# Where the last output wait stands: SyncE's wait moved past the end of the block, the first output moved to ScalarE's queue

## The chip, the cores and the metric

One core of a Trainium2 chip runs the kernel. The metric is device time in microseconds (us), the median of several executions. The *span* is the time from the program's first instruction to its last; the steps that the runtime adds behind the program are called its ending here.

## The reference, cut to what matters

The same decode attention runs twice, on inputs A and B (8 sequences, 32 heads, 4096 cached positions, head size 128, bf16), and the two results stand side by side.

```
q = (x @ wq) split into 32 heads
p = softmax(q . k_cache^T / sqrt(128))
o = p . v_cache
out = o (heads joined: 4096) @ wo          # 8 x 1 x 1024
return concatenate([out_A, out_B], axis=-1)   # 8 x 1 x 2048
```

The caches are read once: the page accounts for 1107 MB read from memory and 0.03 MB written.

## The kernel before

SyncE issues every load but the two small inputs x, which ScalarE issues. The last loads are `wo` of A, then `wo` of B in four pieces, so that the last projection can start before all of it is there. For each cache the projection ends in one cast from PSUM (the memory that the matmuls write) into `orow` on VectorE and one 16 KB store. In the code `c` is 0 for A and 1 for B (`NC` is 2); `add` and `dma` enter an operation together with the list of those that it waits for.

```python
        orow = sb("orow", [128, DT], BF16)
# ... make_proj(c), after the matmuls of cache c:
            opEv[c] = add("dve", lambda e: e.tensor_copy(orow[:], proj[:, 0:DT]), [opProj[c]] + outs)
            outs.append(dma(out[:, 0, c * D:(c + 1) * D].rearrange("b (q n) -> q b n", q=NT), orow[0:128:32 // B, :],
                            ("out", 0), [opEv[c]], "sp"))
# ... the end of the program:
        P.run("sp", nc.sync, sems, part=(0, 2))
        block = es.enter_context(nc.Block())

        @block.sync
        def _(eng):
            P.run("sp", eng, sems, part=(2, None))
            eng.wait_ge(sems[("out", 0)], counts[("out", 0)])
# ... the other four engines alike, without a wait
```

Three things matter. `opEv[1]` waits for the first store, because both casts write the same `orow`. The first store goes onto SyncE's queue behind the pieces of `wo`. And SyncE waits for both stores *inside* the block; the end of a block is a barrier over all five engines: none goes on before all have arrived.

## Time and profile before

| | before |
|---|---|
| time, median of 3 runs before the prediction | 2564.28 us (2564.10 to 2564.41) |
| span of the profiled run | 2562.854 us |
| last piece of `wo` landed | 2559.807 us |
| last output landed | 2562.461 us |
| end of the block's barrier, which is the end of the span | 2562.854 us |
| last step of the runtime's ending in the trace | 2564.814 us |

The page first: busy time by engine, the DMA rows over the span in 40 slices, and the DMA queues (packets, MB, share of 16 engines' time).

```profile
span 2562.9 us, 18832 instructions
PE 1118.5 (44%) x7712; PEld 397.1 (15%) x7712; DVE 2170.2 (85%) x1042; ACT 129.9 (5%) x401; POOL 2.6 (0%) x15
...
DMA  9999999999999999999999999999999999999999
GB/s 425 427 438 430 437 431 437 431 437 431 436 432 435 433 435 433 435 433 433 435 430 435 432 436 432 436 431 436 432 436 432 436 432 435 432 435 433 434 433 394
...
q1 hardware_dynamic: 19512, 1107.34, 99.9%
...
q10 hardware_dynamic: 32, 0.03, 0.0%
```

The DMA engines are busy for at least nine tenths of every slice: the kernel is bound by its loads. Queue 1 is SyncE's, queue 10 ScalarE's, which carries only the two inputs x. A change that leaves the loads alone can move only the ends.

The end of the chain of waits (start us, us, what):

```profile
2520.56 39.25 DMA ring<-in_B_wo_dram
2559.81 0.04 issue
2559.85 0.36 PE proj L431 x4
2560.21 0.02 issue
2560.24 0.42 DVE orow L435
```

The timeline of the last stretch (start us, us, engine, line, operation):

```profile
2559.22 0.97 PE L431 MATMUL proj<-ring,on_sb 128*32 128x256 bf16 x16 [0.28 <-DMA ring<-in_B_wo_dram]
2559.85 0.15 PEld L431 LDWEIGHTS proj<-ring,on_sb 128*32 128x32 bf16 x4 [0.32 <-DMA ring<-in_B_wo_dram]
2560.24 0.42 DVE L435 CAST orow<-proj 128x256 bf16<-128x256 f32 x1 [13.59 <-PE proj L431]
2560.69 0.54 SPq L208 DMA_DIRECT2D out_dram<-orow  x1
```

And SyncE's own waits from 2540 us on (us in total, times, longest):

```profile
SPq L208 <- DVE orow L435: 39.0, 2, 25.7
SPq L162 <- DMA out_dram<-orow: 1.2, 1, 1.2
SPq L162 <- PEq L162: 0.2, 1, 0.2
```

Line 208 is the helper that issues DMAs; line 162 stands for the end of the block. The reader is to see a strict sequence: last piece of `wo`, four matmuls, cast, store, 1.2 us of waiting for the store, and *then* the barrier (0.2 us of waiting in it). The views above stop at the program's last instruction. The trace's semaphore record goes on. It lists when each semaphore, the counter by which engines and transfers signal each other, was updated; no view of `prof` prints it (us, semaphore; 111 counts the outputs, 2 belongs to the runtime):

```
2561.647 sem 111      2562.402 2562.407 2562.416 2562.461 sem 111
2563.093 2563.127 2563.334 2563.378 2563.402 2563.507 2563.546 2563.580 2563.627 sem 2
  (the semaphores are reset)
2564.457 2564.491 2564.529 2564.573 2564.597 2564.695 2564.733 2564.767 2564.814 sem 2
```

Each store updates its semaphore once and then four times more. The Trainium skill says why in "DMA: Bandwidth & Descriptors", section "Why a DMA increments its semaphore by 16 and not by 1": a copy runs on the largest number of engines, up to 16, that divides the slowest dimension of both its sides. Here these are 32 and 4, so four engines. By the same section each engine adds one when its data have landed, and the issuing sequencer writes the remaining count immediately. The trace agrees in the number of updates: one at 2561.647, four later. It does not record their sizes.

The nine steps on semaphore 2 are what the skill's page "Runtime: NRT & Kernel Launch", section "The ~15µs preamble/postamble breakdown", calls a sync barrier, "the actual serpentine across 5 engines", at 44 ns a hop and about 355 ns in all. Nine steps fit a signal that passes over five engines and back, with the fifth step as the turn; the e5 runs below bear this out. The last nine steps of this trace take 357 ns, with single hops of 24 to 98 ns. The first nine take 534 ns, mostly because the third comes 207 ns after the second instead of 38.

### The profile page before, as it was taken

To read this page: it belongs to the slowest core of one execution; us is meant where nothing else is said; L and a number is where in the kernel's file an instruction comes from. 1 tells how busy PE (TensorE), PEld (TensorE's weight loads), DVE (VectorE), ACT (ScalarE), POOL (GpSimd) and SP (SyncE) were. 2 spreads that over 40 slices of the span, in tenths; PEclk is the share of its full clock that TensorE was granted. 3 is DMA by queue.
4 is the path that set the end of the run, shared out by engine and by line. 5 is a ranking of instruction groups with operands and counts; after the bars stand their busy time and mean duration, and the time that the engine had idled before them with its cause. 6 is when DMAs were issued, how large, how long until landed. Compare 5 with 4: busy or idle time off the path is not lost.

```text
span 2562.9 us, 18832 instructions
## 1 busy us (share of the span) xinstructions
PE 1118.5 (44%) x7712; PEld 397.1 (15%) x7712; DVE 2170.2 (85%) x1042; ACT 129.9 (5%) x401; POOL 2.6 (0%) x15
## 2 busy tenths in 40 slices
PE   2443443443443444444444434444444444434435
PEld 1111111111111111111111111111111111111112
DVE  3898898898898898898898888888988988988983
ACT  1100000000000000000000000000000000000000
POOL 0000000000000000000000000000000000000000
PEclk7676776677766766766766767666666767667676
DMA  9999999999999999999999999999999999999999
GB/s 425 427 438 430 437 431 437 431 437 431 436 432 435 433 435 433 435 433 433 435 430 435 432 436 432 436 431 436 432 436 432 436 432 435 432 435 433 434 433 394
DMA packets 19555, 1107.51 MB, mean 432 GB/s; under 512 B 2185, under 2 KB 2249, under 8 KB 2521
## 3 DMA queue, kind: packets, MB, share of 16 engines
q1 hardware_dynamic: 19512, 1107.34, 99.9%
q8 instruction: 7, 0.11, 0.0%
q10 hardware_dynamic: 32, 0.03, 0.0%
q14 instruction: 4, 0.02, 0.0%
HBM read 1107.33 MB, written 0.03 MB: 432 GB/s over the span
## 4 chain that ended last, share of the span: by engine, by line
DMA 52%; DVE 28%; issue 16%; PE 4%; ACT 0%; DVEq 0%; SPq 0%; ACTq 0%
DMA ring<-in_A_k_cache_dram 25%; DMA ring<-in_B_k_cache_dram 25%; DVE ring L330 10%; DVE ring L335 10%; PE red L345 4%; DVE s_sb L353 4%; DVE PM L370 3%; DMA ring<-in_B_wo_dram 2%; DVE rmax L359 1%; DVE rtmp L360 0%; ACT PM L291 0%; DVEq L135 0%; PE o L285 0%; DVE ngm L363 0%; SPq L208 0%
## 5 line engine op out<-in xcount | busy, mean ns | idle before, releaser
L330 DVE TENSOR_TENSOR ring<-ring,qbc 128x8192 bf16<-128x8192 bf16 x256 | 1131.0, 4418 | 309.8 <-DMA ring<-in_B_k_cache_dram 153.0
L345 PE MATMUL red<-ring,ident 128*128 128x512 bf16 x2048 | 782.4, 551 | 1391.1 <-DVE ring L335 1391.1
L335 DVE TENSOR_TENSOR ring<-ring 128x4096 bf16<-128x4096 bf16 x256 | 581.4, 2271 | 0.0
L345 PEld LDWEIGHTS red<-ring,ident 128*128 128x128 bf16 x2048 | 238.8, 127 | 1842.5 <-DVE ring L335 1493.3
L353 DVE TENSOR_REDUCE s_sb<-red 128x64 f32<-128x1024 f32 x256 | 311.1, 1215 | 3.7 <-PE red L345 3.7
L382 PE MATMUL pv<-ring,PM 128*32 128x512 bf16 x4096 | 273.3, 414 | 4.6 <-DVE PM L370 4.6
L370 DVE TENSOR_TENSOR PM<-pe,own_h 128x2048 bf16<-128x2048 bf16 x64 | 146.1, 2284 | 0.7 <-ACT pe L365 0.7
L382 PEld LDWEIGHTS pv<-ring,PM 128*32 128x32 bf16 x4096 | 103.6, 104 | 187.8 <-issue 114.5
L319 ACT ACTIVATE qbc<-misc 128x128 bf16<-128x128 f32 x64 | 17.8, 278 | 1092.5 <-PE misc L317 1092.5
L365 ACT ACTIVATE pe<-s_sb,ngm 128x256 bf16<-128x256 f32 x64 | 32.5, 508 | 468.2 <-DVE ngm L363 468.2
L390 ACT ACTIVATE accS<-pv 128x512 bf16<-128x512 f32 x64 | 38.2, 597 | 350.4 <-PE pv L382 350.4
L399 PEld LDWEIGHTS o<-accS,E 128*32 128x32 bf16 x1024 | 31.3, 100 | 49.7 <-issue 48.5
L399 PE MATMUL o<-accS,E 128*32 128x32 bf16 x1024 | 38.1, 185 | 0.7 <-ACT accS L390 0.7
L405 ACT ACTIVATE o_sb<-o 32x32 f32 (+1 forms) x64 | 11.9, 186 | 451.9 <-PE o L399 451.3
L359 DVE TENSOR_REDUCE rmax<-s_sb 128x1 f32<-128x256 f32 x64 | 26.9, 420 | 2.2
L435 DVE CAST orow<-proj 128x256 bf16<-128x256 f32 x2 | 0.8, 424 | 28.0 <-PE proj L431 28.0
L431 PE MATMUL proj<-ring,on_sb 128*32 128x256 bf16 x256 | 12.8, 379 | 16.3 <-DMA ring<-in_A_wo_dram 9.3
L305 DVE COPY qT<-misc 128x64 bf16<-128x64 bf16 x8 | 3.5, 435 | 18.5 <-PE misc L301 18.5
L312 ACT ACTIVATE qst<-qT 128x128 bf16 (+1 forms) x64 | 18.7, 293 | 2.0 <-DVE qT L305 2.0
L360 DVE TENSOR_SCALAR rtmp<-half,rmax 128x32 f32<-128x32 f32 x64 | 15.4, 241 | 2.3
L363 DVE TRANSPOSE_TENSOR_REDUCE ngm<-rtmp 128x1 f32<-128x32 f32 x64 | 13.5, 212 | 2.2
L317 PE MATMUL misc<-ident,qst 128*128 128x128 bf16 x64 | 14.8, 232 | 0.9 <-ACT qst L312 0.9
(33 smaller groups left out, 66.6 us busy)
## 6 DMA issues: line engine op xcount, KB each, us to landing
ring<-in_B_wo_dram SPq DMA_DIRECT2D x1, 5120.0 KB, 33.2
ring<-in_B_wo_dram SPq DMA_DIRECT2D x1, 2048.0 KB, 37.7
ring<-in_B_wo_dram SPq DMA_DIRECT2D x1, 768.0 KB, 39.1
ring<-in_A_k_cache_dram SPq DMA_DIRECT2D x32, 39.9
ring<-in_A_v_cache_dram SPq DMA_DIRECT2D x32, 27.8
ring<-in_B_k_cache_dram SPq DMA_DIRECT2D x32, 39.8
ring<-in_B_v_cache_dram SPq DMA_DIRECT2D x32, 27.9
ring<-in_B_wo_dram SPq DMA_DIRECT2D x1, 256.0 KB, 39.3
```

Source lines behind the costliest of these rows:

```text
L312: return e.activation(qst[:, n % 2, :].rearrange("p (j m) -> p j m", m=MP), from_.unsqueeze(2).to_broadcast([128, HQ, MP]), ACTF.Copy)
L319: opQbc[n] = add("act", lambda e: e.activation(qbc[:, n % 2, :], misc[:, 0:Dh], ACTF.Copy), [opQb[n], _at(opMul, NR * (n - 2) + NR - 1)])
L330: opMul[s] = add("dve", lambda e: e.tensor_tensor(v, v, qbc[:, n % 2, :].unsqueeze(1).to_broadcast([128, CT, Dh]), ALU.mult), [opT[("k", n ...
L335: return add("dve", lambda e: e.tensor_tensor(v[:, :, 0:64], v[:, :, 0:64], v[:, :, 64:128], ALU.add), [opMul[s]])
L345: i = e.matmul(dst, ident[:], v[:, g, :, j, :], start=(j == 0), stop=(j == 3))
L353: opRed[s] = add("dve", lambda e: e.tensor_reduce(s_sb[:, n % 2, r * CT:(r + 1) * CT], red_ps[s % 2][:, :].rearrange("p (t w) -> p t w", w ...
L359: m = add("dve", lambda e: e.tensor_reduce(rmax[:], s_sb[:, n % 2, :], AX.X, ALU.max), [opRed[NR * n + NR - 1]])
L365: opExp[n] = add("act", lambda e, at: e.activation(pe[:], s_sb[:, n % 2, :], ACTF.Exp, bias=ngm[:, n % 2:n % 2 + 1], scale=scale, accum_ou ...
L370: opPM[n] = add("dve", lambda e: e.tensor_tensor(PM[:], pe[:].unsqueeze(2).to_broadcast([128, T, HQ]), own_h[:].unsqueeze(1).to_broadcast( ...
L382: i = e.matmul(pv_ps[32 * q:32 * (q + 1), :], PM[:, t:t + 4, :].rearrange("p t j -> p (t j)"), v[:, t * Dh:(t + 4) * Dh], start=(g == 0), ...
L390: opAcc[n] = add("act", lambda e: e.activation(accS[:], pv_ps[:], ACTF.Copy), [opPV[n], _at(opExt, n - 1)])
L399: x = e.matmul(to, E[:, i, PH - 1 - u:PH - 1 - u + MB], accS[:, i * 128 + H * u:i * 128 + H * (u + 1)], start=(i == 0 and u == 0), stop=(i ...
```

## The change

The intent: let the block's barrier run while the outputs are in flight, and keep the first output off the load queue.

```diff
-        orow = sb("orow", [128, DT], BF16)
+        orow = sb("orow", [128, NC, DT], BF16)
@@
-            opEv[c] = add("dve", lambda e: e.tensor_copy(orow[:], proj[:, 0:DT]), [opProj[c]] + outs)
-            outs.append(dma(out[:, 0, c * D:(c + 1) * D].rearrange("b (q n) -> q b n", q=NT), orow[0:128:32 // B, :],
-                            ("out", 0), [opEv[c]], "sp"))
+            opEv[c] = add("dve", lambda e: e.tensor_copy(orow[:, c, :], proj[:, 0:DT]), [opProj[c]])
+            outs.append(dma(out[:, 0, c * D:(c + 1) * D].rearrange("b (q n) -> q b n", q=NT), orow[0:128:32 // B, c, :],
+                            ("out", 0), [opEv[c]] if c == NC - 1 else [opEv[c], opT[("wo", NC - 1, len(wo_cuts) - 1)]],
+                            "sp" if c == NC - 1 else "act"))
@@
-        block = es.enter_context(nc.Block())
-        @block.sync
-        def _(eng):
-            P.run("sp", eng, sems, part=(2, None))
-            eng.wait_ge(sems[("out", 0)], counts[("out", 0)])
+        with nc.Block() as block:
+            @block.sync
+            def _(eng):
+                P.run("sp", eng, sems, part=(2, None))
# ... the other engines only indented
+        nc.sync.wait_ge(sems[("out", 0)], counts[("out", 0)])
```

More of the change, by code (lines that the diff above doesn't have):

```diff
@@ L507, in _build_kernel, with _ @@
         P.run("sp", nc.sync, sems, part=(0, 2))
-        block = es.enter_context(nc.Block())
-        @block.sync
-        def _(eng):
-            P.run("sp", eng, sems, part=(2, None))
-            eng.wait_ge(sems[("out", 0)], counts[("out", 0)])
-        @block.tensor
-        def _(eng):
-            P.run("pe", eng, sems, loops["pe"])
-        @block.scalar
-        def _(eng):
-            P.run("act", eng, sems, loops["act"])
-        @block.vector
-        def _(eng):
-            P.run("dve", eng, sems, loops["dve"])
-        @block.gpsimd
-        def _(eng):
-            P.run("pool", eng, sems)
+        with nc.Block() as block:
+            @block.sync
+            def _(eng):
+                P.run("sp", eng, sems, part=(2, None))
+            @block.tensor
+            def _(eng):
+                P.run("pe", eng, sems, loops["pe"])
+            @block.scalar
+            def _(eng):
+                P.run("act", eng, sems, loops["act"])
+            @block.vector
+            def _(eng):
+                P.run("dve", eng, sems, loops["dve"])
+            @block.gpsimd
+            def _(eng):
+                P.run("pool", eng, sems)
+        nc.sync.wait_ge(sems[("out", 0)], counts[("out", 0)])
 def bass_concat_heads__mha_block_cached__mha_block_cached__decode_kernel(
```

## The prediction

> **What bounds the kernel.** DMA. The page's DMA row is 9 in all 40 slices, 432 GB/s over the span; its queue part gives the SyncE load queue 99.9% of the 16 engines' time. VectorE is 85% busy, TensorE 44%. The cache loads are not touched, so over 2500 us of the 2562.9 us span should come back unchanged. Only the last microseconds can move.
>
> **The tail before (timeline, chain of waits, semaphore record).** The last piece of wo lands at 2559.81. TensorE ends at 2560.21; the VectorE cast runs 2560.24 to 2560.66; SyncE issues the second output at 2560.69 (541 ns). Its packets move at 2561.87 to 2562.10; the last increment comes at 2562.46. Only then does SyncE reach the end of the block, whose all-engine barrier takes until 2562.87: 0.4 us after the landing. The runtime's own ending follows: semaphore-2 steps from 2563.09, 34 ns apart with one late step of 207 ns, turning at 2563.40, then resets, the last step at 2564.81. The Trainium skill, "Runtime: NRT & Kernel Launch", section "The ~15µs preamble/postamble breakdown", calls this a sync barrier, a serpentine over five engines at 44 ns a hop, then resets. The trace agrees (357 ns for the last one).
>
> **What the change does.**
> 1. The wait for the outputs goes past the block's barrier, which now runs in the shadow of the output's flight: SyncE is free of the issue at 2561.23, the barrier should be over near 2561.6, the landing stays near 2562.46. Gain on the critical path about 0.4 us. The other engines enter the runtime's ending early and wait there; the late step (0.17 us) is probably hidden too. Estimate 0.2 us more, seen in the time, not in the span.
> 2. The first output goes out on ScalarE's queue after wo has landed: issue near 2559.83, landing near 2561.7, before the second's 2562.46. Before, it was issued at 2546.68 behind wo on 4 of the 16 engines and landed at 2559.11, 0.7 us before the last piece of wo. So wo was not held up by it; taking it away (32 packets of 27 ns) gains nothing.
> 3. orow has two halves, so VectorE no longer waits for the first output. That wait was over at 2559.14, before the matmuls ended: gain nothing.
> 4. Possible cost: two outputs are issued within 0.9 us, and the second may be issued cold (the first took 696 ns, the second 541). At most about 0.2 us.
>
> **Sum.** Span 2562.9 to about 2562.5. Time 2564.28 - 0.4 - 0.2 + 0.1 = about 2563.8 us, 0.02% faster: within 2% nearly for certain. The three runs before lie within 0.31 us, but other runs can shift by more than the gain, so the range is wider than the argument: 2562.6 to 2564.9. Chances: faster 0.005, within 2% 0.99, slower 0.005.
>
> **What would show each step.** (1) The block's barrier steps before the output's last increment; the span ends with SyncE's wait, near 2562.5; from wo's last landing to the span's end 2.7 us instead of 3.05. (2) A ScalarE issue of the output near 2559.8; queue 10 has more packets than its 32; wo's last landing within 0.3 us of before. (3) The cast still follows TensorE's end by 0.02 us. (4) The second output's issue to landing stays 1.8 us.
>
> **What would make it wrong.** The first output landing last; the barrier outlasting the flight; an instruction fetch after the block's end; a load stream that differs by a microsecond from run to run, which would swamp 0.5 us.

The semaphore-2 steps are not all 34 ns apart, as the prediction has it: apart from the late one they lie 24 to 105 ns apart before. Its figure of 44 ns a hop is the page's for the barrier in front of the kernel.

## The result, and the profile after

A ratio is the mean time of one kernel's runs over that of the other's of the same rounds, so not quite the ratio of the medians quoted.

| | before | after |
|---|---|---|
| median, 6 runs each | 2564.32 us (2564.10 to 2564.41) | 2563.52 us (2563.39 to 2563.80) |
| ratio, 95% interval | | 0.9997 [0.9984, 1.001] |
| profiled run: time | 2564.63 | 2563.80 |
| span | 2562.854 | 2562.555 |
| last step of the runtime's ending | 2564.814 | 2563.984 |

The interval of the ratio includes 1. The two sets of six runs do not overlap, though, and the difference of 0.80 us came back in a later set of runs (first experiment below).

The page after. Queue 10 now carries 68 packets; its 36 more are the first output's 32 pieces of 512 bytes and four semaphore updates. The load row is as before.

```profile
span 2562.6 us, 18832 instructions
...
DMA  9999999999999999999999999999999999999999
GB/s 425 427 438 430 436 432 436 432 436 432 436 432 436 430 437 430 436 432 435 432 435 431 435 433 433 435 433 435 432 436 432 435 433 435 433 435 433 435 433 394
...
q1 hardware_dynamic: 19476, 1107.32, 99.9%
...
q10 hardware_dynamic: 68, 0.05, 0.0%
```

The end of the chain of waits after:

```profile
2520.46 39.30 DMA ring<-in_B_wo_dram
2559.75 0.04 issue
2559.80 0.36 PE proj L431 x4
2560.16 0.03 issue
2560.19 0.42 DVE orow L435
```

The timeline after:

```profile
2559.80 0.15 PEld L431 LDWEIGHTS proj<-ring,on_sb 128*32 128x32 bf16 x4 [0.31 <-DMA ring<-in_B_wo_dram]
2559.84 0.65 ACTq L208 DMA_DIRECT2D out_dram<-orow  x1
2560.19 0.42 DVE L435 CAST orow<-proj 128x256 bf16<-128x256 f32 x1 [12.91 <-PE proj L431]
2560.64 0.69 SPq L208 DMA_DIRECT2D out_dram<-orow  x1
```

SyncE's waits after (line 509 is the block's end, line 531 the wait behind it):

```profile
SPq L208 <- DVE orow L435: 39.7, 1, 39.7
SPq L531 <- DMA out_dram<-orow: 0.6, 1, 0.6
SPq L509 <- PEq L509: 0.2, 1, 0.2
```

The chain up to the cast is the same. SyncE's own issue of the store takes 0.69 us instead of 0.54. The wait for the store has shrunk from 1.2 to 0.6 us: the rest of the flight is now covered by the barrier. The semaphore record after:

```
2560.904 sem 111 (ScalarE's store)   2561.658 2561.664 2561.670 2561.706 (its landing)
2561.712 sem 111 (SyncE's store)     2562.455 2562.467 2562.470 2562.522 (its landing)
2562.255 2562.289 2562.496 2562.540 2562.677 2562.721 2562.759 2562.793 2562.842 sem 2
2563.627 2563.661 2563.699 2563.742 2563.766 2563.865 2563.903 2563.937 2563.984 sem 2
```

Four steps of the runtime's ending, the late one (the third) among them, now come *before* the last output has landed or just after (2562.540 against 2562.522). The fifth comes once SyncE's wait is over. In all ten profiled runs the measured time is the last step less 0.18 to 0.19 us, so the whole difference, of one trace of each kernel, can be split along this record:

| piece | before | after | difference |
|---|---|---|---|
| last piece of `wo` landed | 2559.807 | 2559.754 | -0.05 |
| from there to the last output's landing | 2.654 | 2.768 | +0.11 |
| from there to the end of the span | 0.393 | 0.033 | -0.36 |
| from there to the last step of the ending | 1.960 | 1.429 | -0.53 |
| last step | 2564.814 | 2563.984 | -0.83 |

Of the 0.393 us before, 0.05 pass until SyncE is released (2562.510), 0.13 until it reaches the block's end (2562.639), and 0.21 in the barrier. The last two now run while the output is in flight; of the first, 0.03 are left.

### The profile page after: what moved, and what is told of

Read it like the earlier page. It is cut to its first block, busy times and chain, and to the rows that moved or that the text cites. A ratio compares the mean times of both kernels' runs of the same rounds, so it can differ in the third digit from the quotient of the medians.

```text
span 2562.6 us, 18832 instructions
## 1 busy us (share of the span) xinstructions
PE 1118.0 (44%) x7712; PEld 397.3 (16%) x7712; DVE 2170.6 (85%) x1042; ACT 129.8 (5%) x401; POOL 2.6 (0%) x15
## 4 chain that ended last, share of the span: by engine, by line
DMA 52%; DVE 28%; issue 16%; PE 4%; ACT 0%; another core or an unknown queue 0%; DVEq 0%; SPq 0%
DMA ring<-in_A_k_cache_dram 25%; DMA ring<-in_B_k_cache_dram 25%; DVE ring L330 10%; DVE ring L335 10%; PE red L345 4%; DVE s_sb L353 4%; DVE PM L370 3%; DMA ring<-in_B_wo_dram 2%; DVE rmax L359 1%; DVE rtmp L360 0%; ACT PM L291 0%; PE o L285 0%; DVEq L135 0%; DVE ngm L363 0%
```

## The experiments

The theory (T in the expectations) is that moving the wait brings all of the gain, about half of it inside the block's barrier and the other half in the runtime's ending, and that the ScalarE queue brings nothing and costs 0.1 us at the second store's issue. The rivals: the first result was drift; the quieter load queue brings part of the gain (Q); two issues close together collide, and this is why the store's issue got longer (K); the gain in the ending has nothing to do with which engine waits (U).

The trace's times of all runs (us). "A" runs from `wo`'s last landing to the last output's landing, "B" from there to the last step of the ending.

| run | `wo` landed | A | B | last step | median of the timed runs | before, same rounds |
|---|---|---|---|---|---|---|
| before | 2559.807 | 2.654 | 2.353 | 2564.814 | 2564.32 (6) | |
| after | 2559.754 | 2.768 | 1.462 | 2563.984 | 2563.52 (6) | 2564.32 (6) |
| a0_after_again | 2559.763 | 2.777 | 1.466 | 2564.006 | 2563.55 (5) | 2564.36 (9) |
| e1_wait_past_block | 2559.663 | 2.662 | 1.466 | 2563.791 | 2563.60 (5) | 2564.36 (9) |
| e2_act_queue_only | 2559.719 | 2.776 | 2.310 | 2564.805 | 2564.62 (5) | 2564.36 (9) |
| e3_act_early | 2559.516 | 2.771 | 1.510 | 2563.797 | 2563.61 (5) | 2564.36 (9) |
| e4_sp_late | 2559.758 | 2.654 | 1.465 | 2563.877 | 2563.56 (5) | 2564.34 (9) |
| e5_wait_on_tensor | 2559.571 | 2.762 | 1.783 | 2564.116 | 2563.92 (5) | 2564.34 (9) |
| e5_wait_on_gpsimd | 2559.460 | 2.764 | 2.015 | 2564.239 | 2564.17 (5) | 2564.34 (9) |
| e5_wait_on_scalar | 2559.805 | 2.773 | 1.633 | 2564.211 | 2563.89 (5) | 2564.34 (9) |

All outputs were correct. `wo`'s landing differs by 0.35 us among the runs: this is the spread of the load stream, and it is why A and B tell more than a single time. B has a spread of its own: the pause between the ninth and the tenth step of the ending was 0.83 us before and in e3 and 0.79 us in the other eight runs, whatever the arrangement. That is why B is 0.05 us longer in e3 than after, and 0.04 us longer before than in e2.

### a0_after_again: the changed kernel once more

No edit.

> The changed kernel again, as the yardstick on this chip. All theories: 0.7 to 0.9 us under the kernel before of the same rounds; if it is within 0.3 us of it, the first result was drift between runs and nothing needs explaining.

Measured: 2563.55 us against 2564.36, 0.81 us less. A and B repeat within 0.01 us. It was not drift.

### e1_wait_past_block: the wait alone

```diff
 # the kernel before, but:
-            eng.wait_ge(sems[("out", 0)], counts[("out", 0)])      # inside @block.sync
+        nc.sync.wait_ge(sems[("out", 0)], counts[("out", 0)])      # after the block
```

> Only the wait is moved past the block; the first output stays on the SyncE queue, early, and orow stays one buffer. Theory T (all of the gain is the wait's): 0.8 to 0.95 us under the kernel before, so as fast as the changed kernel or 0.1 us faster, because the second output's issue stays at about 540 ns instead of 688. Rival Q (the quiet load queue brings part of the gain): less than 0.5 us under the kernel before.

Measured: 2563.60 us, 0.76 us under the kernel before, slightly short of the expected 0.8 but far from Q's 0.5. B is 1.466 us, as with the whole change. The store's issue is short again, and A with it (2.662):

```profile
2560.10 0.42 DVE L435 CAST orow<-proj 128x256 bf16<-128x256 f32 x1 [14.41 <-PE proj L431]
2560.55 0.54 SPq L208 DMA_DIRECT2D out_dram<-orow  x1
...
SPq L530 <- DMA out_dram<-orow: 0.6, 1, 0.6
```

(The last line is from SyncE's waits; line 530 is the wait behind the block.)

The wait brings the gain alone. (The edit also writes the block as a `with` statement, as the changed kernel does. e2 has that too, without the gain, so this form is not the cause.) That A is 0.11 us shorter than after did not show in the median, 0.05 us *above* that of the changed kernel; with a spread of 0.2 to 0.45 us in five runs this cannot be told apart.

### e2_act_queue_only: the queue and the two halves alone

```diff
 # the changed kernel, but:
+                eng.wait_ge(sems[("out", 0)], counts[("out", 0)])  # inside @block.sync again
-        nc.sync.wait_ge(sems[("out", 0)], counts[("out", 0)])
```

> Only the first output is moved (ScalarE's queue, after wo, two halves of orow); SyncE still waits inside the block. Theory T: 0 to 0.15 us SLOWER than the kernel before (second issue about 690 ns). Rival Q: at least 0.3 us faster.

Measured: 2564.62 us, 0.26 us slower by the medians and 0.15 us by the means (2564.54 against 2564.39): by the means at the edge of the expected 0.15, by the medians past it. The ratio is 1.0001. B is back at 2.310 us, A is the changed kernel's 2.776, and SyncE's wait for the output is the old one:

```profile
SPq L509 <- DMA out_dram<-orow: 1.2, 1, 1.2
...
2560.60 0.70 SPq L208 DMA_DIRECT2D out_dram<-orow  x1
```

(The first line is from SyncE's waits, the second from the timeline.) Moving the first output gains nothing by itself; Q has fallen.

### e3_act_early: ScalarE's store without its wait for wo

```diff
-                            ("out", 0), [opEv[c]] if c == NC - 1 else [opEv[c], opT[("wo", NC - 1, len(wo_cuts) - 1)]],
+                            ("out", 0), [opEv[c]],
```

> The changed kernel, but ScalarE issues the first output as soon as the cast is done (about 2547 us) and does not wait for wo. Tells two things. (a) Why SyncE's output issue takes 688 ns in the changed kernel: if it is cold (SyncE's first output), it stays near 690; if it collides with ScalarE's issue 0.8 us earlier, it falls to about 540 and the time falls by 0.1 us. (b) Whether output packets on a second queue hold up wo: wo's last landing should stay within 0.2 us of 2559.8; a hold-up shows as a later one.

Measured: 2563.61 us, the changed kernel's time. ScalarE now issues at 2546.58, nearly 14 us before SyncE, and SyncE's store still takes as long:

```profile
2546.58 0.65 ACTq L208 DMA_DIRECT2D out_dram<-orow  x1
...
2560.40 0.70 SPq L208 DMA_DIRECT2D out_dram<-orow  x1
```

So the longer issue is no collision with ScalarE's: K has fallen. (b) `wo`'s last piece landed at 2559.516, 0.28 us earlier than the expected 2559.8 and outside the band I gave, but not a hold-up. The store itself landed at 2555.998, ahead of the last pieces of `wo`; on SyncE's queue, behind them, it had landed at 2559.112. Making the store wait for `wo` protects nothing that could be measured here.

### e4_sp_late: the late first output on SyncE's queue

```diff
-                            "sp" if c == NC - 1 else "act"))
+                            "sp"))
```

> The changed kernel, but the late first output (it still waits for the last piece of wo) is issued by SyncE and not by ScalarE. Theory C (the first output that SyncE issues takes about 690 ns, whenever it comes, and the next about 540): the first takes 690, the second 540, and from wo's last landing to the last output's landing 2.65 to 2.7 us; time equal to the changed kernel within 0.15 us. Rival K (two issues within 1 us collide): the second stays at 690 or more and the interval at 2.77 us or more.

Measured: 2563.56 us. The first store took 692 ns, the second, 0.80 us after the first one's start, 541 ns, and A is 2.654 us. The tile view of `orow` (ns, shortest, median and longest):

```profile
L208 SPq DMA_DIRECT2D out_dram<-orow x2: 541/616/692, 2559.8 to 2560.6; - x2
```

SyncE's first store took 688 to 696 ns wherever it stood (early, late, with or without ScalarE's), and its second 540 or 541 ns. The price of moving the first store to ScalarE is thus that SyncE's last store becomes its first. The cause of the difference inside the sequencer stays open.

### e5: the last wait on another engine

Three kernels, each the changed kernel with one word changed; the shown diff is the first.

```diff
-        nc.sync.wait_ge(sems[("out", 0)], counts[("out", 0)])
+        nc.tensor.wait_ge(sems[("out", 0)], counts[("out", 0)])   # the others: nc.gpsimd, nc.scalar
```

> The changed kernel, but TensorE holds the last wait instead of SyncE. Theory S (the runtime's ending begins with a chain of steps over the engines, TensorE first and SyncE at the turn; what SyncE's wait leaves to do is only the way back): now the whole way out comes after the landing too, so from the output's last landing to the last step of the ending 1.65 to 1.85 us instead of 1.46; 0.2 to 0.35 us slower than the changed kernel. Rival U (each engine gains the same, it only matters that the wait is out of the block): 1.4 to 1.55 us, time equal within 0.1 us.

> The changed kernel, but GpSimd holds the last wait. Theory S, with GpSimd as the engine of the late third step (207 ns): that late step now comes after the landing: 1.75 to 1.95 us from the output's last landing to the last step of the ending, 0.3 to 0.5 us slower than the changed kernel and so slower than with TensorE. If GpSimd is not the late one: 1.55 to 1.75. Rival U: 1.4 to 1.55 us.

> The changed kernel, but ScalarE holds the last wait. Theory S, with ScalarE second in the chain: a little less than with TensorE, 1.6 to 1.8 us from the output's last landing to the last step of the ending. If ScalarE is the late third step, 1.75 to 1.95. Rival U: 1.4 to 1.55 us.

Measured, the first nine steps of the runtime's ending beside the end of the wait (us):

```
wait on   wait ends   steps
SyncE     2562.555    2562.255 .289 .496 .540 | .677 .721 .759 .793 .842
ScalarE   2562.616    2562.306 | .735 .773 .817 .841 .946 .985 2563.019 .066
TensorE   2562.412    | 2562.608 .642 .681 .725 .748 .852 .892 .926 .973
GpSimd    2562.265    2561.959 .993 | .802 .846 .869 .974 2563.013 .047 .094
```

The bar stands before the step of the engine that held the wait, the first one after its wait ended: each engine holds up exactly its own place in the chain and all that follow. TensorE stands first, ScalarE second, GpSimd third, SyncE fifth, at the turn. VectorE is left for the fourth place, which no run tried. U has fallen: B is 1.783 us with TensorE, 1.633 with ScalarE and 2.015 with GpSimd, against 1.462 with SyncE, and the medians are 2563.92, 2563.89 and 2564.17 us. GpSimd was expected at 1.75 to 1.95 us and came out above. In time it is 0.62 us slower than the changed kernel (a0, other rounds) where 0.3 to 0.5 was expected, TensorE 0.37 where 0.2 to 0.35 was. From the end of its wait to its step it takes 0.54 us, where ScalarE and SyncE take 0.12 and TensorE 0.20. It is also the late third step of the kernel before: there, and in the changed kernel, the third step comes 0.57 us after GpSimd's last instruction in the block (2562.767 to 2563.334, 2561.929 to 2562.496). With TensorE last, the late step is gone (39 ns instead of 207), because GpSimd had arrived in time. Why GpSimd is slow to arrive stays open.

No version tried is measurably faster than the changed kernel. e1 and e4 have the shortest tails (A and B together 4.13 and 4.12 us, against 4.23 for the changed kernel), at equal medians.

## Why the prediction was right

It said 2563.8 us (2562.6 to 2564.9); the median was 2563.52. The range is so wide that the time before, 2564.32, lies in it too, so that the median fell inside says little. Of the gain, 0.5 us was forecast and 0.80 measured. What speaks for the argument is its steps, each read from the trace. Point by point:

- *Bound by the loads, only the tail can move.* Right: the DMA rows are the same, and `wo` landed 0.05 us earlier than before.
- *The barrier goes into the shadow of the flight, about 0.4 us.* Right: 0.393 us from landing to the end of the span became 0.033. I had put the barrier's end near 2561.6; it came near 2562.0, because the store's issue ended 0.10 us later than assumed and SyncE's drain (the instruction with which it enters the barrier) took 0.42 us with the store just issued (7 ns before, when the store had landed). It was still hidden.
- *0.2 us more in the runtime's ending.* The mechanism was right, the size was not. This is the mis-sized term of the sum: it measured 0.53 us instead of 0.2. I had counted only the late third step. Before, from the end of the span to the turn of the serpentine it took 0.548 us (2562.854 to 2563.402): 0.239 us from there to the first step and 0.309 us of steps outward. After, SyncE alone must still arrive: 0.122 us (2562.555 to 2562.677). That is 0.43 us. The e5 runs show that this depends on SyncE standing at the turn: with the wait on another engine, its end and the turn lay 0.23 to 0.60 us apart. The rest, 0.10 us, lies behind the turn (1.412 to 1.307 us to the last step). Of that, 0.06 us is the step right behind it: 105 ns before, in e2 and in the e5 runs to within 1 ns, 43 or 44 ns in all five where SyncE waits behind the block. The other 0.04 us is the pause named under the table, which varies by itself and is no gain of the change.
- *The first output on ScalarE's queue gains nothing.* Right (e2). *The two halves of orow gain nothing.* e1 keeps one buffer and has the same gain; in its trace VectorE's wait for the first store is over at 2559.20, before the matmuls end.
- *Possible cost at the second store, about 0.1 us in the sum.* Right: +0.11 us, and it is the first-store cost (e3, e4), not the nearness of two issues.
- Of the signs I named, the interval from `wo`'s landing to the end of the span is 2.80 us and not 2.7, and issue to landing 1.88 us and not 1.8, both by those 0.11 us.

## What to carry to other kernels

A wait that only guards the end of the program can stand after the last barrier and not before it, so that barrier and flight overlap; in this kernel, the only one tried, that alone was worth 0.8 us, of which more than half lay behind the program's own span, where the usual views do not look. Which engine holds that wait matters: put it on the one that the runtime's ending needs last (SyncE here; GpSimd gave back 0.6 us of it). Moving the small store off the full load queue brought nothing here, where the store was not what held the loads up, and it made SyncE's last store its first, which took 0.15 us longer to issue than a second one.

## What the Trainium skill lacked or had wrong

- "Runtime: NRT & Kernel Launch", section "The ~15µs preamble/postamble breakdown": it names the serpentine but not the engines' places, nor that the engine that holds the last wait decides how much of it is exposed. The runs show TensorE first, ScalarE second, GpSimd third, SyncE at the turn, and 1.46 to 2.02 us from the landing to the last step, by the engine that waits.
- The same section gives the closing sync barrier about 1.5 us and does not say from where. Here the last of its nine steps came 0.77 us after the end of the span before (2562.854 to 2563.627) and 0.29 us after it with the change (2562.555 to 2562.842). The nine steps took 534 ns before, 168 ns of them GpSimd's late arrival (207 instead of 39 ns, the step with TensorE waiting).
- No page that I read has it that SyncE's first store takes longer to issue than its next: 688 to 696 ns against 540 or 541, for the same 16 KB. Whether ScalarE does the same no run here shows (its only store took 652 ns).
- "DMA: Bandwidth & Descriptors", section "Latency and other measured facts", gives about 600 ns to the first byte for this way of issuing, without saying from when. Counted from the end of the issue, the trace agrees: 0.64 us before (2561.231 to 2561.869) and 0.60 us after (2561.328 to 2561.924). Counted from its start it is 1.18 and 1.28 us, so the time of the issue itself has to be added.
- The same page, section "Anatomy of one DMA — SWDGE (gpsimd) path", says of the GpSimd path that most of the fixed cost is the write receipt. On the SyncE path the store before had 1.18 us in front of its first packet and 0.34 us between its last packet and its last increment (2562.122 to 2562.461), of 1.77 us in all.
